# Weight loads by whole rows, the Gelu table load placed elsewhere, and two more MLP products copied out raw

## The chip, the cores and the metric

The kernel runs on one core of a Trainium2 chip. The metric is the device time of one execution in microseconds (us); a kernel's time is the median of its runs. TensorE is PE, VectorE is DVE, ScalarE is ACT, GpSimd is POOL, and SP is the engine whose queue issues nearly all the transfers.

## The reference

The reference is a transformer layer with a recurrent memory, followed by an MLP. The sequence of 2048 tokens is worked off in 64 segments of 32 tokens, and each segment sees eight memory rows that the segment before produced.

```
# per segment s (8 memory rows + 32 tokens, 512 wide, 32 heads of 128)
h = concat(mem, layernorm(x)[s])
q, k, v = h @ Wq, h @ Wk, h @ Wv
p = softmax(mask(q @ k.T * scale));  o = (p @ v) @ Wo
mem = o[:8];  out[s] = o[8:]
# whole sequence, F = 1792
h = x + out
h2 = h + gelu(layernorm(layernorm(h)) @ w1 + b1) @ w2 + b2
```

Wq, Wk and Wv are each 512 x 4096 in bf16, so that one of their rows has 8192 bytes.

## The kernel before

**Staging.** WQ, WK, WV and WO (4 MB each) are loaded once and stay in SBUF while the 64 segments run one after another. WQ lies in SBUF as 128 partitions x 4 blocks x 4096 columns: block `c` holds rows `128 c` to `128 c + 127` of the matrix. A projection contracts over the four blocks, and it is made in two halves: half `r = 0` yields heads 0 to 15 (columns 0 to 2047), and half `r = 1` heads 16 to 31. So a half needs the same 2048 columns of all four blocks. Each half is 16 matmuls, four for each block.

**The opening.** Segment 0 is written out by hand in the table `START`: the V projections of the tokens of blocks 0 and 1 (`("B", "V", ...)`, operand `hB`) and of the memory part (`"V"`, operand `hT`), then K in the same way, then Q in the order Q of block 0 half 0 (`hB`), `Q0` (`hT`), Q of block 0 half 1 (`hB`), `Q1` (`hT`), and then the scores `SC0` and `SC1`. The loads are issued by SP in the order WV, WK, WQ, WO. `load_w` cuts each of the three projection matrices into four transfers of 1 MB.

**The steady part.** From segment 1 on, tables fix PE's order by segment. PE is the engine that has work nearly all the time.

**The MLP.** When the last segment is done, the MLP runs over four groups `k` of 512 tokens. `w1_first` makes the 14 products (`fc` 0 to 13) with W1 of the first group, partly in the last segments, into PSUM banks 4 and 5 in turn. While ACT still needs its Exp tables, such a product is copied out of PSUM as it is ("raw") into a buffer `gT0`, and `gelu_late` applies Gelu in place later; the other products go through Gelu on the way out of PSUM (the line of `w1_first`'s `activation`). `RAW` is the number of products that are copied raw. The compiler puts an `ACT_TABLE_LOAD` ahead of the first Gelu. The buffers of `gT0` are re-used tiles, so a trace shows them as `xn`, `hT`, `kq`, `VSB`, `QTB`, `VBD` and, for fc 12 and 13, `hT` again.

The products with W2 accumulate in the four banks of `quad`, one for each 128 tokens. At the end of a group, DVE adds the residual to each bank and writes the output row block (`WV<-quad,WV`, since the old WV holds these buffers). `p2_norm(k)` normalizes the rows of group `k` on DVE (`WV<-WQ,agg,rst`, four instructions); it waits until `p2_load(k)` has brought them from memory (`WQ<-h_mid`). `p2_T(k)` transposes them by DMA.

**What sets the order of the engines.** PE's order is the order of the program. For the other engines a planner sorts all operations by their rank, which is the length of what depends on them, plus a bonus from the table `BONUS` by name, and inserts each at the earliest place that a table of costs gives. So a change of one name's bonus, or of one duration, can put later operations of ACT, DVE and SP in another order. What an operation may wait for follows from its `reads` and `writes` keys; `("WQ", r, c)` is the key of half `r` of block `c`.

Of the kernel before, what the change touches and what calls it, by code (L numbers as in the profile page):

```python
# [22 lines left out]
TABLE = 1.28  # L23
# [7 lines left out]
RECORD = ()  # L31
KEEP = True
HOIST = 24
LATE, RAW, LEAD = 0, 10, 199
PIECES = (0, 4, 8, 11, 14)
HALVES = ("kq", "KA", "QT", "ZCm", "VS", "nmc", "EC", "rsc", "PC", "PTC", "OTm", "KB", "QTB", "VSB")
BONUS = {"": 3.88, "EC0": 19.37, "EC0@a1": -40, "EC0@a2": 0, "EC0@a3": 2.13, "EC0@m0": 4.48, "EC0@m1": 40, "EC0@m2": 0, "EC0@m3": -7.71,
# [466 lines left out]
DC = 4  # L504
# [4 lines left out]
FC = F // P  # L509
# [43 lines left out]
def t_dve(n):  # L553
    return 0.16 + 1.042e-3 * n
# [10 lines left out]
def build_kernel(nc, A_x, A_mem0, A_Wq, A_Wk, A_Wv, A_Wo, B_w1, B_b1, B_w2, B_b2, out):  # L565
# [3 lines left out]
    with st:  # L569
        def sb(name, shape, dt=BF16):  # L570
            return st.enter_context(nc.sbuf_tensor(name, shape, dt))
# [54 lines left out]
        cneg = sb("cneg", [P, 1], F32)  # L626
        b2bc = sb("b2bc", [P, D])
        m0 = b2bc[0:MEM, :]
        b1n = sb("b1n", [FC, P])
        b1t = sb("b1t", [P, FC], F32)  # L630
# [39 lines left out]
        for sl in range(2):  # L670
            for i in range(4):
# [20 lines left out]
             reads=["maskA"], writes=["maskA"])  # L692
# [9 lines left out]
        def load(fn, kb, writes):  # L702
            chain.append(S.dma(fn, kb, writes=writes))
        chain, spread = [], {}

        def load_w(W, wd, key):
            for r in range(2):
                for c0 in (0, 2):
                    load(lambda e, r=r, c0=c0: e.dma_start(W[:, c0:c0 + 2, r * 2048:(r + 1) * 2048], wd[:, c0:c0 + 2, r * 2048:(r + 1) * 2048]),  # L709
                         1024, [(key, r, c0), (key, r, c0 + 1)])  # L710

        def first(fn, kb, writes):
            S.dma(fn, kb, writes=writes, eng="act")
# [2 lines left out]
        first(lambda e: e.dma_start(b1n[:], b1_d), 4, ["b1n"])  # L716
        load_x(1, first)
        load_w(WV, wv_d, "WV")
        load_w(WK, wk_d, "WK")
        load_w(WQ, wq_d, "WQ")  # L720
        for g in range(4):
            for a in range(2):
# [292 lines left out]
        exps = []  # L1015
# [127 lines left out]
        def view(base, off, shape, dt=BF16):  # L1143
            b = base[:]
            n = 1
            for x_ in shape[1:]:
                n *= x_
            m = 2 if dt == F32 else 1
            flat = bass.AP(b.tensor, b.offset + off, [[b.ap[0][0], shape[0]], [1, m * n]])
            if dt == F32:  # L1150
                flat = flat.bitcast(F32)
            names = " ".join("a%d" % i for i in range(len(shape) - 1))
            return flat.rearrange("p (%s) -> p %s" % (names, names), **{"a%d" % i: shape[i + 1] for i in range(len(shape) - 2)})
# [5 lines left out]
        gT = view(WQ, 0, [P, FC, SBT])  # L1159
# [70 lines left out]
        def w1_first(fc, bank, raw=False):  # L1230
            p = fc // 2
            views, keys = homes[p]
            for cc in range(DC):
                v, c0, _ = [w for w in views if w[1] <= cc < w[2]][0]
                S.op("pe", lambda e, v=v, c=cc - c0, cc=cc: e.matmul(ps[bank][:, 0:SBT], v[:, c, (fc % 2) * P:(fc % 2 + 1) * P], hnT0[:, cc, :], start=(cc == 0),  # L1235
                                                                     stop=(cc == DC - 1), skip_group_check=True),
                     reads=keys + [("hnT", "first", t) for t in range(TBS)], writes=[("ps", bank)], dur=0.215, mode=MF, ni=2)
            g, gkeys = gT0_home[p]
            g = g[:, fc % 2, :]
            if raw:  # L1240
                S.either(copy2(g, ps[bank][:, 0:SBT], 512), reads=[("ps", bank)], writes=[("gT0", fc)] + gkeys)
                return
            S.op("act", lambda e: e.activation(g, ps[bank][:, 0:SBT], ACTF.Gelu_apprx_tanh, bias=b1t[:, fc:fc + 1], scale=1.0),
                 reads=[("ps", bank), "b1t"], writes=[("gT0", fc)] + gkeys, after=exps + gelus[:1], dur=0.69)

        gelus = []

        def gelu_late(fc):
            g, gkeys = gT0_home[fc // 2]
            g = g[:, fc % 2, :]  # L1250
            o = S.named(S.op("act", lambda e: e.activation(g, g, ACTF.Gelu_apprx_tanh, bias=b1t[:, fc:fc + 1], scale=1.0),
                     reads=["b1t"], writes=[("gT0", fc)] + gkeys, after=exps + gelus[:1], dur=0.66 if gelus else 0.66 + TABLE), "gl")
            gelus.append(o)

        def gT_of(k, fc):
# [249 lines left out]
        for fc in range(6, FC):  # L1505
            w1_first(fc, (4, 5)[fc % 2], fc < RAW)
            rest.get(fc, lambda: None)()
            if fc == 7:
                for i in range(6):
                    gelu_late(i)  # L1510
            if fc >= 9 and fc < RAW:
                for i in range(6, fc + 1) if fc == 9 else (fc,):
                    gelu_late(i)
        nat(NTB - 1)
        p2_res(0)
# [2 lines left out]
        for k in range(NSB):  # L1518
# [13 lines left out]
            for t in range(TBS):  # L1532
                tb, split = k * TBS + t, is_last(k, t)
                for i in range(2 if split else 1):
                    for fc in range(FC - lag, FC):
                        p2_w2t(k, fc, t, i if split else None)
                    c = slice(i * HALF, (i + 1) * HALF) if split else slice(0, D)
                    keys = [("ob", bf, t, i)] if split else [("ob", bf, t, 0), ("ob", bf, t, 1)]
                    src, key = (ps[7][:, 0:HALF], ("ps", 7)) if i else (quad[:, t, c], ("ps", t))
                    S.op("dve", lambda e, t=t, bf=bf, c=c, src=src: e.tensor_tensor(ob[:, bf, t, c], src, hb[:, bf, t, c], ALU.add),  # L1540
                         reads=[key, ("hb", bf, t)], writes=keys, after=used["WV"], dur=t_dve(c.stop - c.start))
# [6 lines left out]
def bass_sequential_preLN__memory_aug_recurrent_mem_tr__mixer_channel_mlp__prompt_kernel(  # L1548
    nc: bass.Bass,
    A_x: bass.AP,  # L1550
    A_mem0: bass.AP,
    A_Wq: bass.AP,
    A_Wk: bass.AP,
    A_Wv: bass.AP,
    A_Wo: bass.AP,
    A_seg_len,
    B_x: bass.AP,
    B_w1: bass.AP,
    B_b1: bass.AP,
    B_w2: bass.AP,  # L1560
    B_b2: bass.AP,
    out: bass.AP,
):
    assert int(A_seg_len) == SEG
    build_kernel(nc, A_x, A_mem0, A_Wq, A_Wk, A_Wv, A_Wo, B_w1, B_b1, B_w2, B_b2, out)
# [33 lines left out]
```

## Time and profile before

| what | value |
|---|---|
| median of three runs | 807.16 us (805.53 to 807.7) |
| profiled execution, its own time | 805.57 us |
| span of the profiled execution, first to last instruction | 803.8 us |
| PE busy | 778.6 us, 97% of the span |
| DVE, ACT, POOL busy | 75%, 69%, 11% |
| mean granted TensorE clock | 0.993 |
| chain that ended last | PE 92%, DMA 2%, SP's queue 2%, DVE 2%, ACT 1% |

The profiled execution took 805.57 us, of which 1.8 us lie outside the span. It is 1.6 us shorter than the median of the three runs. PE is busy for nearly the whole span, so what the other engines do costs time only where PE waits; the page's row of slices shows where PE is not full: the first two of 40 slices (0 to 40 us) and the last one.

### The profile page before, as it was taken

Reading aid. Unit: us, or ns where it says so; the run is one execution under the profiler, and the core shown is the slowest. Engines: PE = TensorE matmul, PEld = TensorE weight load, DVE = VectorE, ACT = ScalarE, POOL = GpSimd, SP = SyncE. Lnnn points to the kernel's source line nnn. Section 1 sums busy time; section 2 is a strip of 40 time slices with the busy share of each in tenths; the row PEclk is TensorE's granted clock in tenths of the full one; section 3 lists DMA queues with packets and bytes.
Section 4 is the critical chain, followed back from the end, with each engine's and each line's share of the span. In section 5 each row is a group of like instructions: output and inputs, shape, how many; then the busy total and the mean of one; then the engine's idle time right before and its main releaser. Section 6 shows DMA issues by size and latency. Waiting matters only on the chain.

```text
span 803.8 us, 46836 instructions
## 1 busy us (share of the span) xinstructions
PE 778.6 (97%) x21699; PEld 424.4 (53%) x20879; DVE 600.1 (75%) x1846; ACT 557.5 (69%) x1579; POOL 89.7 (11%) x211
## 2 busy tenths in 40 slices
PE   2899999999999999999999999999999999999998
PEld 1455555555555555555555555555555555644444
DVE  3277878888888888888888888888888888733311
ACT  1556777777777777777777777777777777773342
POOL 5012000010001010101010101000000000020700
PEclk9979999999999999999999999999999999999999
DMA  8962010111111111202020202010203111074300
GB/s 340 392 194 30 4 35 8 40 23 37 26 36 26 33 29 27 36 19 41 19 43 16 48 12 50 13 37 20 50 24 57 45 44 54 21 230 129 86 27 26
DMA packets 67091, 48.77 MB, mean 61 GB/s; under 512 B 28996, under 2 KB 63308, under 8 KB 66892
## 3 DMA queue, kind: packets, MB, share of 16 engines
q1 hardware_dynamic: 66560, 45.50, 21.1%
q8 instruction: 166, 2.72, 1.4%
q14 instruction: 33, 0.27, 0.1%
q10 hardware_dynamic: 332, 0.27, 0.1%
HBM read 31.08 MB, written 8.13 MB: 49 GB/s over the span
## 4 chain that ended last, share of the span: by engine, by line
PE 92%; DMA 2%; SPq 2%; DVE 2%; ACT 1%; issue 0%; DVEq 0%; ACTq 0%
PE ps L798 43%; PE ps L1085 15%; PE ps L547 8%; PE quad L1467 6%; PE ps L1453 5%; PE ps L1114 3%; PE quad L996 3%; DMA WQ<-in_A_Wq_dram 2%; PE quad L1057 2%; SPq L709 2%; PE ps L1027 2%; PE ps L1235 1%; PE ps L965 1%; PE quad L965 1%; PE quad L1000 1%; DVE TT L1097 0%
## 5 line engine op out<-in xcount | busy, mean ns | idle before, releaser
L1085 PE MATMUL ps<-WO,OT 128*32 128x256 bf16 x4224 | 141.2, 276 | 0.1
L798 PE MATMUL ps<-WQ,hT 128*32 128x512 bf16 x1864 | 131.5, 380 | 0.9 <-DVE hT L1091 0.5
L798 PE MATMUL ps<-WV,hT 128*32 128x512 bf16 x1364 | 125.5, 382 | 0.0
L798 PE MATMUL ps<-WK,hT 128*32 128x512 bf16 x1700 | 123.7, 380 | 0.1
L817 ACT ACTIVATE kq<-ps 128x512 bf16<-128x512 f32 x160 | 95.4, 596 | 35.9 <-PE ps L798 29.0
L1085 PEld LDWEIGHTS ps<-WO,OT 128*32 128x32 bf16 x4224 | 101.4, 97 | 26.5 <-ACT OT L816 5.5
L816 ACT CAST kq<-ps 128x512 bf16<-128x512 f32 x162 | 94.7, 585 | 20.3 <-PE ps L798 13.7
L816 ACT CAST OT<-quad 128x128 bf16<-128x128 f32 (+1 forms) x192 | 85.1, 443 | 26.0 <-PE quad L1000 17.6
L841 DVE STREAM_TRANSPOSE KALL<-kq 128x256 f32<-128x256 f32 x160 | 71.1, 444 | 15.3 <-ACT kq L816 11.8
L798 PEld LDWEIGHTS ps<-WQ,hT 128*32 128x32 bf16 x1864 | 49.7, 97 | 60.1 <-issue 18.2
L863 POOL COPY ZC<-QTB 128x256 bf16<-128x256 bf16 x64 | 25.5, 399 | 477.8 <-PE ps L965 455.5
L798 PEld LDWEIGHTS ps<-WK,hT 128*32 128x32 bf16 x1700 | 45.9, 96 | 57.2 <-issue 14.9
L547 PE MATMUL ps<-WV,hT 128*32 128x512 bf16 x684 | 67.7, 379 | 0.0
L798 PEld LDWEIGHTS ps<-WV,hT 128*32 128x32 bf16 x1364 | 38.8, 97 | 47.1 <-issue 36.9
L841 DVE STREAM_TRANSPOSE QT<-kq 128x256 f32<-128x256 f32 x128 | 57.0, 445 | 7.0 <-ACT kq L817 2.1
L1456 ACT ACTIVATE WQ<-ps,b1t 128x512 bf16<-128x512 f32 x42 | 28.9, 687 | 47.4 <-PE ps L1453 47.4
L1097 DVE STREAM_TRANSPOSE TT<-ps 128x256 f32<-128x256 f32 x66 | 29.6, 449 | 38.3 <-PE ps L1085 38.2
L816 ACT CAST VS<-ps 128x512 bf16<-128x512 f32 x65 | 38.0, 585 | 27.0 <-PE ps L798 26.9
L1540 DVE TENSOR_TENSOR WV<-quad,WV 128x512 bf16<-128x512 f32 (+1 forms) x16 | 10.7, 674 | 47.8 <-PE quad L1467 47.8
L816 DVE CAST VS<-ps 128x512 bf16<-128x512 f32 x63 | 41.7, 663 | 5.6 <-PE ps L798 5.6
L798 PE MATMUL ps<-WQ,hB 128*32 128x512 bf16 x512 | 42.4, 397 | 2.7 <-DMA WQ<-in_A_Wq_dram 2.0
L984 DVE TENSOR_TENSOR PC<-EC,rsc 128x128 bf16<-128x128 f32 x128 | 39.7, 310 | 4.3
(161 smaller groups left out, 1428.6 us busy)
## 6 DMA issues: line engine op xcount, KB each, us to landing
WV<-in_A_Wv_dram SPq DMA_DIRECT2D x4, 1024.0 KB, 10.2
WK<-in_A_Wk_dram SPq DMA_DIRECT2D x4, 1024.0 KB, 16.1
WQ<-in_A_Wq_dram SPq DMA_DIRECT2D x4, 1024.0 KB, 22.6
WO<-in_A_Wo_dram SPq DMA_DIRECT2D x8, 512.0 KB, 9.3
v_last<-VSB SPq DMA_DIRECT2D x60, 64.0 KB, 2.8
VBD<-v_last SPq DMA_DIRECT2D x60, 64.0 KB, 3.0
h_mid<-xr SPq DMA_DIRECT2D x16, 128.0 KB, 1.8
WK<-in_B_w_dram SPq DMA_DIRECT2D x4, 512.0 KB, 4.6
```

Of the source, the lines that this page charges most:

```text
L547: return e.add_instruction(mybir.InstMatmult(name="I-%d" % (4000000 + _kept[0]), engine=mybir.EngineType.PE, start_tensor_calc=start, stop ...
L798: ins = e.matmul(o, l, m, start=(k == 0), stop=(k == DC - 1), tile_position=(0, 32 * j), skip_group_check=True)
L816: return {"act": (lambda e: e.copy(out, src), t_act(n, ps_)), "dve": (lambda e: e.tensor_copy(out, src), 0.16 + 1.042e-3 * n * fast)}
L817: return {"act": (lambda e: e.mul(out, src, scale_), t_act(n, ps_)), "dve": (lambda e: e.tensor_scalar(out, src, scale_, None, ALU.mult), ...
L841: S.op("dve", lambda e: e.transpose(out, src), reads=[("kq", i)], writes=[key], dur=t_dve(256) + 0.02, after=after)
L863: S.op("pool", lambda e: e.tensor_copy(dst, src), reads=[("QTB", bk % 2, q) for q in range(2)], writes=[("ZCb", par)], dur=0.45)
L984: S.op("dve", lambda e: e.tensor_tensor(PC[:, r].rearrange("p t a -> p a t"), EC[:, r], bc, ALU.mult), reads=[("EC", r), ("rsc", r)], writ ...
L1085: ins = e.matmul(ps[bank][32 * j:32 * j + 32, 0:256], lhs(slot(h)), wo_cols(h, b), start=(k == 0), stop=(k == 15), tile_position=(0, 32 * ...
L1097: S.op("dve", lambda e: e.transpose(tt.rearrange("p c q t -> p (c q t)"), ps[bank][:, 0:256]), reads=[("ps", bank)], writes=[("TT", par)], ...
L1453: ins = e.matmul(ps[bank][:, 0:SBT], W1[:, cc, fc * P:(fc + 1) * P], hnT_of(k)[:, cc, :], start=(cc == 0), stop=(cc == DC - 1))
L1456: S.op("act", lambda e: e.activation(gT[:, fc, :], ps[bank][:, 0:SBT], ACTF.Gelu_apprx_tanh, bias=b1t[:, fc:fc + 1], scale=1.0), reads=[(" ...
L1467: S.op("pe", lambda e: e.matmul(quad[:, t, :], lhs, W2[:, fc, :], **flags), reads=[("W2", part_of(fc))] + gT_keys(k, fc), writes=[("ps", t ...
```

## The change

Three things change. First, `load_w` issues, for each of WV, WK and WQ, four transfers of whole rows, one for each block `c`, in place of four transfers of half rows. The bytes and the number of transfers are the same. Second, `RAW` goes from 10 to 12: the products fc 10 and 11 are copied raw into `VBD`, and their Gelu follows in place, after the Gelus of the others in the program. Third, the first late Gelu, ahead of which the table load stands, gets a name of its own, `gl0`, with a bonus of 10 where it had -40.

```diff
-LATE, RAW, LEAD = 0, 10, 199
+LATE, RAW, LEAD = 0, 12, 199
...
-... "gl": -40,
+... "gl": -40, "gl0": 10,
...
         def load_w(W, wd, key):
-            for r in range(2):
-                for c0 in (0, 2):
-                    load(lambda e, r=r, c0=c0: e.dma_start(W[:, c0:c0 + 2, r * 2048:(r + 1) * 2048], wd[:, c0:c0 + 2, r * 2048:(r + 1) * 2048]),
-                         1024, [(key, r, c0), (key, r, c0 + 1)])
+            for c in range(DC):
+                load(lambda e, c=c: e.dma_start(W[:, c, :], wd[:, c, :]), 1024, [(key, r, c) for r in range(2)])
...
-                     reads=["b1t"], writes=[("gT0", fc)] + gkeys, after=exps + gelus[:1], dur=0.66 if gelus else 0.66 + TABLE), "gl")
+                     reads=["b1t"], writes=[("gT0", fc)] + gkeys, after=exps + gelus[:1], dur=0.66 if gelus else 0.66 + TABLE), "gl" if gelus else "gl0")
...
-            if fc >= 9 and fc < RAW:
-                for i in range(6, fc + 1) if fc == 9 else (fc,):
+            if fc == 9:
+                for i in range(6, 10):
+                    gelu_late(i)
+            if RAW > 10 and fc == FC - 1:
+                for i in range(10, RAW):
                     gelu_late(i)
```

The first place where instructions wait for something else is PE's Q projections in the opening. `dsem12` to `dsem15` are the semaphores of WQ's four transfers, `hB` is the operand of block 0's tokens and `hT` that of the memory part. Before:

```order
L798 MATMUL ps<-WQ,hB 32x512 [waits sem_act]
L798 MATMUL ps<-WQ,hB 32x512 x7
L798 MATMUL ps<-WQ,hB 32x512 [waits dsem13]
L798 MATMUL ps<-WQ,hB 32x512 x7
L798 MATMUL ps<-WQ,hT 32x512 [waits sem_act]
L798 MATMUL ps<-WQ,hT 32x512 x15
L798 MATMUL ps<-WQ,hB 32x512 [waits dsem14]
L798 MATMUL ps<-WQ,hB 32x512 x7
L798 MATMUL ps<-WQ,hB 32x512 [waits dsem15]
L798 MATMUL ps<-WQ,hB 32x512 x7
L798 MATMUL ps<-WQ,hT 32x512 x16
```

And of the changed kernel, whose lines here are two lower:

```order
L796 MATMUL ps<-WQ,hB 32x512 [waits sem_act]
L796 MATMUL ps<-WQ,hB 32x512 x3
L796 MATMUL ps<-WQ,hB 32x512 [waits dsem13]
L796 MATMUL ps<-WQ,hB 32x512 x3
L796 MATMUL ps<-WQ,hB 32x512 [waits dsem14]
L796 MATMUL ps<-WQ,hB 32x512 x3
L796 MATMUL ps<-WQ,hB 32x512 [waits dsem15]
L796 MATMUL ps<-WQ,hB 32x512 x3
L796 MATMUL ps<-WQ,hT 32x512 [waits sem_act]
L796 MATMUL ps<-WQ,hT 32x512 x15
L796 MATMUL ps<-WQ,hB 32x512 x16
L796 MATMUL ps<-WQ,hT 32x512 x16
```

The matmuls stand in the same order. The wait for the fourth transfer stood ahead of the last 24 of these 64 matmuls, and it now stands ahead of the last 52.

The second place is DVE at the end of the MLP's first group. `WV<-quad,WV` is the output of 128 tokens out of a bank of `quad`, `WV<-WQ,agg,rst` is `p2_norm`, here of group 2, and `dsem3` is the semaphore of that group's load. Before:

```order
L1121 TENSOR_TENSOR OTB<-ps,OTB 64x512 [waits sem_act]
L1540 TENSOR_TENSOR WV<-quad,WV 128x512 [waits sem_pe,sem_pool] x4
L1186 TENSOR_SCALAR WV<-WQ,agg,rst 128x512 [waits dsem3]
L1186 TENSOR_SCALAR WV<-WQ,agg,rst 128x512 x3
L1122 TENSOR_TENSOR oBn<-OTB 32x512 [waits dsem90,dsem89,dsem91,dsem88,sem_dve]
```

Of the changed kernel:

```order
L1119 TENSOR_TENSOR OTB<-ps,OTB 64x512 [waits sem_act]
L1541 TENSOR_TENSOR WV<-quad,WV 128x512 [waits sem_pe,sem_pool]
L1184 TENSOR_SCALAR WV<-WQ,agg,rst 128x512 [waits dsem3]
L1184 TENSOR_SCALAR WV<-WQ,agg,rst 128x512 x3
L1541 TENSOR_TENSOR WV<-quad,WV 128x512 [waits sem_pe] x3
L1120 TENSOR_TENSOR oBn<-OTB 32x512 [waits dsem90,dsem89,dsem91,dsem88,sem_dve]
```

The normalization of group 2 with its wait has moved ahead of the last three of the four outputs.

The third place is ACT at the start of the MLP, from the last raw copies on. `QTB` holds the products fc 8 and 9, `VBD` fc 10 and 11; `OT<-quad` is the output of an attention step. Before:

```order
L816 CAST QTB<-ps 128x512 x2
L816 CAST OT<-quad 128x32x24
L1251 ACT_TABLE_LOAD
L1251 ACTIVATE xn<-xn,b1t 128x512 x2
L1251 ACTIVATE hT<-hT,b1t 128x512
L1251 ACTIVATE kq<-kq,b1t 128x512
L1243 ACTIVATE VBD<-ps,b1t 128x512 x2
L1243 ACTIVATE hT<-ps,b1t 128x512 x2
```

Of the changed kernel:

```order
L814 CAST QTB<-ps 128x512 x2
L1249 ACT_TABLE_LOAD
L1249 ACTIVATE xn<-xn,b1t 128x512 x2
L1249 ACTIVATE hT<-hT,b1t 128x512 x2
L1249 ACTIVATE kq<-kq,b1t 128x512
L814 CAST VBD<-ps 128x512 x2
L1241 ACTIVATE hT<-ps,b1t 128x512 x2
```

The copy of `OT` has left ACT (it now stands on DVE, where there was nothing between two groups of transposes), one more late Gelu stands ahead of the copies of fc 10 and 11, and these two are casts. The two Gelus that are missing here come later, behind those of `QTB`.

2 rows, old and new, of the table BONUS are left out of this document.

## The prediction

> **What bounds the kernel now.** I read the page first, then the chain of waits for the opening, then the two places where PE's order meets a changed wait: the Q projections and the start of the MLP. The page says where time can be won or lost at all:
>
> ```profile
> PE 778.6 (97%) x21699; PEld 424.4 (53%) x20879; DVE 600.1 (75%) x1846; ACT 557.5 (69%) x1579; POOL 89.7 (11%) x211
> PE 92%; DMA 2%; SPq 2%; DVE 2%; ACT 1%; issue 0%; DVEq 0%; ACTq 0%
> WQ<-in_A_Wq_dram SPq DMA_DIRECT2D x4, 1024.0 KB, 22.6
> ```
>
> PE has work for 97% of the span and is 92% of the chain; the steady part in between is not touched by the change. DMA and SP's queue make 4%, and both are in the opening. The chain (start, length, what) of the first 50 us:
>
> ```profile
> 18.94 18.43 DMA WQ<-in_A_Wq_dram
> 37.41 1.58 PE ps L798 x24
> 40.87 1.74 PE ps L798 x15
> 45.01 1.71 PE ps L798 x16
> 46.72 1.71 PE ps L1085 x32
> ```
>
> All before 37.4 us hangs on the last piece of WQ: only then do the last 24 Q matmuls run. PE's timeline at that place (start, length, instructions, idle time before):
>
> ```profile
> 29.48 1.91 PE L798 MATMUL ps<-WK,hT 128*32 128x512 bf16 x32
> 31.22 1.91 PE L798 MATMUL ps<-WK,hB 128*32 128x512 bf16 x32
> 32.95 1.04 PE L798 MATMUL ps<-WQ,hB 128*32 128x512 bf16 x16
> 34.84 0.62 PE L798 MATMUL ps<-WQ,hB 128*32 128x512 bf16 x8
> 37.41 0.61 PE L798 MATMUL ps<-WQ,hB 128*32 128x512 bf16 x8 [1.96 <-DMA WQ<-in_A_Wq_dram]
> 37.85 1.12 PE L798 MATMUL ps<-WQ,hT 128*32 128x512 bf16 x16
> ```
>
> PE is idle for 1.96 us. The stages show transfers and clock (length; busy PE, PEld, DVE, ACT, POOL; granted clock, DMA share, GB/s):
>
> ```profile
> 26.00:28.00 2.00, 2.00 (x40) 1.46 (x131) 0.00 (x0) 1.02 (x3) 0.00 (x0) 1.00 1.03 416
> 32.00:34.00 2.00, 2.00 (x44) 0.87 (x36) 1.04 (x3) 1.20 (x3) 0.00 (x0) 1.00 1.02 403
> 38.00:40.00 2.00, 1.30 (x36) 0.46 (x24) 0.81 (x2) 1.47 (x3) 0.74 (x2) 0.67 1.05 344
> 42.00:44.00 2.00, 1.42 (x84) 0.72 (x79) 1.14 (x4) 1.20 (x4) 0.00 (x0) 0.50 1.10 348
> 48.00:50.00 2.00, 2.00 (x44) 1.24 (x40) 0.82 (x3) 0.00 (x0) 0.00 (x0) 0.77 0.79 243
> ```
>
> The transfers run at some 410 GB/s until WQ is in, so the opening is bound by bandwidth. And behind the idle stretch the granted clock is 0.5: 0.67 in 38 to 40 us means from about 38.7 us on, 0.77 in 48 to 50 us means until about 48.9 us. That is 10.2 us, in which 16 matmuls of the chain take 1.71 us, while 32 took 1.74 us before (29.48 to 31.22).
>
> **The change part by part.**
>
> *Rows of 8192 bytes.* WQ's four pieces now end one block each, not one half each. Twelve pieces of 1024 KB at 410 GB/s are 12.58 MB / 410 = 30.7 us. Does a longer row move faster? The nearest rows: pieces with 4 KB rows move at 410 GB/s, WO with 1 KB rows at 348 GB/s (42 to 44 us, when only WO moves). Over 16 engines that is 160 ns for 4 KB and 47 ns for 1 KB, so a line through both gives 37.6 ns per KB and 9.4 ns a piece; 8 KB would take 310 ns, or 422 GB/s. The three matrices then take 29.8 us: **0.9 us earlier**, the last piece at 36.5 us. Bounds: 0 (the rows are cut to 4 KB anyway, the piece lands at 37.4 us) and, for no fixed cost at all, twice as much (1.8 us). The Trainium skill, "DMA: Bandwidth & Descriptors", section "Why small descriptors are slow (HBM only)", names a fixed cost of about 3 cycles a packet beside one cycle per 32 bytes; by it a 4 KB row is 131 cycles and two are 262 against 259, an estimate of 0.3 us, and the sum would come out 0.6 us higher. The rows of this trace show more than twice that fixed cost, so I stay with 0.9 us.
>
> *What is left to do behind the last piece.* Before, half 0 needed two pieces and was done before the wait; 24 matmuls were left. Now the fourth block is needed by half 0 already: 12 matmuls run, and 52 are left. A matmul is 1.74 / 32 = 0.054 us, so 28 more of them cost **1.5 us**, and nothing hides them, since the scores and the softmax follow on Q1 in both kernels. WV and WK also come by blocks now, without harm: WQ's four pieces of 2.56 us ahead of 37.4 us put WK's last piece at 27.2 us at the latest, and PE takes up WK's first block 32 matmuls ahead of the row at 29.48, at 27.7 us.
>
> *The clock.* PE is now idle from about 33.7 us (32.95 and 12 matmuls) to 36.5 us, 2.8 us instead of 1.96. A gap of 1.96 us was enough for 10.2 us at half clock, so I expect the half clock again, and it can come earlier: before the 52 matmuls, not behind the 24. Bounds: none of the extra matmuls slowed, 0; all 52 slowed, 52 x 0.054 = 2.8 us, of which some comes back because the slow stretch then ends earlier. I take a third, **0.9 us**. The Trainium skill, "TensorE: Matmul & The Clock Gate", section "Why this matters for your kernels", says that gaps up to about 3 us are safe; this trace has the clock drop behind 1.96 us, so the measurement decides. Part 1 of the same page of the Trainium skill says that the monitor's window runs free of the kernel's start, which would make the loss differ from run to run; one trace cannot show that.
>
> *The MLP's start.* PE waits here once, for the bank of fc 10:
>
> ```profile
> 711.54 1.90 PE L1235 MATMUL ps<-hnT,hT 128*128 128x512 bf16 x8
> ...
> 713.74 0.60 PE L1235 MATMUL ps<-hnT,xT 128*128 128x512 bf16 x2 [0.30 <-ACT VBD L1243]
> ...
> 708.29 0.81 ACT L816 CAST OT<-quad 128x768 bf16<-128x768 f32 x1
> 709.11 1.28 ACT L1251 ACT_TABLE_LOAD   x1
> ...
> 711.79 0.70 ACT L1251 ACTIVATE hT<-hT,b1t 128x512 bf16<-128x512 bf16 x1
> 712.40 0.71 ACT L1251 ACTIVATE kq<-kq,b1t 128x512 bf16<-128x512 bf16 x1
> 713.02 1.39 ACT L1243 ACTIVATE VBD<-ps,b1t 128x512 bf16<-128x512 f32 x2
> ...
> 720.40 0.58 ACT L1120 COPY OTB<-ps 64x512 f32<-64x512 f32 x1
> ...
> 724.11 0.59 PE L1467 MATMUL quad<-WK,VBD 128*128 128x512 bf16 x2
> ```
>
> The `OT` copy leaves ACT and the table load comes 0.7 us earlier, but one more Gelu (0.6 us from row to row) stands ahead of fc 10's copy, which is a cast of 0.58 us and no Gelu of 0.7 us. So the bank comes free 0.2 us earlier: **-0.2 us** (at best the whole 0.3). The two Gelus that were put off follow `QTB`'s. ACT was through with all Gelus at 720.4 us; it now has two casts more (1.2 us) and the `OT` copy less (0.8 us), so it is through at 720.8 us, and PE wants `VBD` at 724.1 us: hidden, with 3 us of cover.
>
> *The moved normalization.* The rows of group 2 and the outputs (DVE), the load (SP) and PE's next products:
>
> ```profile
> 726.11 0.69 DVE L1540 TENSOR_TENSOR WV<-quad,WV 128x512 bf16<-128x512 f32 x1 [0.17 <-PE quad L1467]
> ...
> 727.83 0.69 DVE L1540 TENSOR_TENSOR WV<-quad,WV 128x512 bf16<-128x512 f32 x1 [0.17 <-PE quad L1467]
> 730.31 1.38 DVE L1186 TENSOR_SCALAR WV<-WQ,agg,rst 128x512 bf16<-128x512 bf16 x4 [1.78 <-DMA WQ<-h_mid]
> ...
> 725.75 0.45 SPq L1180 DMA_DIRECT2D WQ<-h_mid  x1
> ...
> 732.06 1.03 PE L1467 MATMUL quad<-WK,WQ 128*128 128x512 bf16 x4
> 732.92 1.03 PE L1453 MATMUL ps<-WQ,WK 128*128 128x512 bf16 x4
> ```
>
> The load is issued at 725.75 us and lands at 730.3 us in either kernel: what SP does ahead of it is the same. DVE now does one output, waits for the load, normalizes (1.38 us, until 731.7) and only then frees the other three banks of `quad`, each 0.69 us behind the one before: 732.4, 733.1, 733.75 us. PE's four products, one for each bank, begin at 732.06 us less the 0.2 won above, 0.215 us apart (four from 732.06 to 732.92), so it wants the fourth bank at 732.5 us and gets it at 733.75. **+1.2 us** (from 0.4, if the load comes 0.8 us earlier, to 2, if it comes later). SP's group transposes now stand ahead of three stores, which nobody waits for. The last block's rows and POOL's residuals are late by 1.5 us too:
>
> ```profile
> 745.58 8.93 POOL L1192 TENSOR_TENSOR WV<-WQ,b2bc 128x512 f32<-128x512 bf16 x8
> 752.18 0.69 DVE L1540 TENSOR_TENSOR WV<-quad,WV 128x512 bf16<-128x512 f32 x1 [0.17 <-PE quad L1467]
> ```
>
> Four of the eight, 4.5 us, are due before 752.18 us; they end at 750.05 us, so 2.1 us of cover are left.
>
> *The sum.* -0.9 + 1.5 + 0.9 - 0.2 + 1.2 = **+2.5 us**. On the profiled execution, 805.57 us, that is 808.1 us; this one is 1.6 us below the median, and on the median of 807.16 us it is **809.7 us**, 0.3% slower. A difference of 0.3% (2.4 us) is about what a measurement of this kernel can tell from no change, as its runs from 805.53 to 807.7 us show.
>
> **The rivals.**
>
> *The clock isn't dropped* (not slower). If PE, with its gap at another place, still counts as busy enough, the opening runs at full clock. The chain's three rows at half clock (1.74 + 1.71 + 1.71 us) then take half, 2.6 us less at most; part of the first row lies beside the softmax and would turn into a wait, so I take 2.2 us. That comes off the time before, and the forecast's +0.9 us falls away: 809.7 - 0.9 - 2.2 = **806.6 us**. It decides if a gap of 2.8 us leaves the clock up. Against it: a gap of 1.96 us did drop it. For it: the gap now begins 1.7 us earlier, and one trace says little on where the limit lies. By the skill's rule on gaps this would be the usual case; the trace bears that out badly. Chance 0.20.
>
> *The rows bring nothing* (the change doesn't do what it says). The 8 KB rows are cut to 4 KB or move no faster: the 0.9 us are gone, the gap is 3.7 us, and the slow stretch takes in all 52 matmuls, 2.8 us in place of the 0.9 counted, of which some 0.9 come back at its end. 809.7 + 0.9 + 1.0 = **811.6 us**. For it: no row that I quote moves 8 KB at a time from SP's queue. Chance 0.20.
>
> *The normalization doesn't stall PE.* If the load lands by 729 us, the banks come free in time: 809.7 - 1.2 = **808.5 us**. Against it: SP's queue ahead of the load is unchanged. Chance 0.10.
>
> **How the numbers follow.** The forecast has 0.50; its own range, from the bounds of the clock (0 to 2 us) and of the stall (0.4 to 2 us), is 808 to 811.6 us, about half on each side of 0.3%: 0.28 slower, 0.22 within. The first rival gives 0.08 faster (where the rows gain their 1.8 us too: 805.7 us, and the stall stays out: 804.5 us) and 0.12 within; the second 0.20 slower; the third 0.10 within. So faster 0.08, within 0.44, slower 0.48. The range reaches down to 805.7 us, that end of the first rival, and up to 812.5 us, 0.9 us above the second for a load that lands later.
>
> **What would show it.** Right: PE's Q matmuls wait once, ahead of the 13th, for 2.5 to 3 us until about 36.5 us; transfers at 420 GB/s until then; a stretch at clock 0.5 that begins before 38.7 us; no wait for `VBD` at 713 us or one under 0.15 us; and a PE wait of about 1.2 us at `quad<-WK,WQ`, with DVE idle for some 4 us between the first output and the normalization. Wrong: 410 GB/s or less, a clock of 1.0 through 50 us, or no wait of PE at the second group's first W2 products.

## The result and the profile after

The changed kernel takes 804.29 us (median of 18 runs, 802.47 to 807.41), the kernel before 806.33 us (18 runs, 805.08 to 807.7). The ratio is 0.9974, with a 95% interval of 0.9964 to 0.9984: some 2.0 us faster (1.3 to 2.9). The forecast was 2.5 us slower, and the time lies below its range. (The 809.7 us were counted from 807.16 us, the median of three runs; 0.8 us of the distance is that the median of 18 is 806.33 us.) The profiled execution took 803.95 us, with a span of 802.2 us.

The page of the changed kernel (busy times, packets by size):

```profile
PE 775.9 (97%) x21699; PEld 423.1 (53%) x20880; DVE 600.7 (75%) x1847; ACT 558.0 (70%) x1580; POOL 90.1 (11%) x211
DMA packets 65555, 48.77 MB, mean 61 GB/s; under 512 B 28996, under 2 KB 63308, under 8 KB 63820
```

And the packet row of the kernel before:

```profile
DMA packets 67091, 48.77 MB, mean 61 GB/s; under 512 B 28996, under 2 KB 63308, under 8 KB 66892
```

The three matrices are 12 MB: 3072 packets of 4 KB before, 1536 of 8 KB after. The total fell by just 1536, and the packets of 2 KB or more but under 8 KB by 3072. So the 8 KB rows are moved whole. PE is busy for 2.7 us less (778.6 to 775.9 us) with the same instructions, since less of them fall into a stretch at half clock, as the windows show. The transfers are faster too; two stretches of the windows (length; busy PE, PEld, DVE, ACT, POOL; granted clock, DMA share, GB/s), first of the kernel before, then of the changed kernel, there with two more:

```profile
2.00:12.00 10.00, 0.30 (x4) 0.11 (x4) 1.79 (x3) 1.55 (x2) 6.32 (x31) 1.00 0.95 346
12.00:30.00 18.00, 13.71 (x173) 8.22 (x360) 4.96 (x7) 7.03 (x16) 4.53 (x6) 1.00 1.02 409
```

```profile
2.00:12.00 10.00, 0.30 (x4) 0.11 (x4) 1.79 (x3) 1.55 (x2) 6.32 (x31) 1.00 0.97 393
12.00:30.00 18.00, 13.00 (x164) 7.82 (x347) 4.54 (x7) 6.71 (x15) 4.57 (x6) 1.00 1.01 421
42.00:44.00 2.00, 1.56 (x89) 1.34 (x78) 1.29 (x5) 1.21 (x5) 0.00 (x0) 0.60 1.10 348
44.00:46.00 2.00, 2.00 (x32) 1.06 (x28) 0.69 (x2) 0.53 (x2) 0.00 (x0) 0.55 1.10 350
```

From 12 us on the rate goes from 409 to 421 GB/s; ahead of that, where ACT's queue brings rows of x beside the weights, it goes from 346 to 393 GB/s. The last two rows show WO's 1 KB rows at 348 to 350 GB/s, as before, and a granted clock of 0.60 and 0.55: half clock for 1.6 + 1.8 = 3.4 us, where it was 10.2 us before. PE's timeline in the opening of the changed kernel:

```profile
33.47 0.82 PE L796 MATMUL ps<-WQ,hB 128*32 128x512 bf16 x12
35.34 0.40 PE L796 MATMUL ps<-WQ,hB 128*32 128x512 bf16 x4 [1.05 <-DMA WQ<-in_A_Wq_dram]
43.89 1.96 PE L796 MATMUL ps<-WQ,hB 128*32 128x512 bf16 x16
47.30 0.62 PE L1083 MATMUL ps<-WO,OT 128*32 128x256 bf16 x16
```

PE takes up the 13th Q matmul at 35.34 us, after a single wait as predicted, but one of 1.05 us and not of 2.5 to 3; it was 37.41 us for the last piece before, so the piece comes 2.1 us earlier. The opening ends when DVE transposes the output of segment 0 (`TT`). That row before and after, and the same row of the last segment:

```profile
49.89 0.45 DVE L1097 STREAM_TRANSPOSE TT<-ps 128x256 f32<-128x256 f32 x1 [1.15 <-PE ps L1085]
701.68 0.45 DVE L1097 STREAM_TRANSPOSE TT<-ps 128x256 f32<-128x256 f32 x1 [2.27 <-PE ps L1085]
```

```profile
47.97 0.45 DVE L1095 STREAM_TRANSPOSE TT<-ps 128x256 f32<-128x256 f32 x1
700.09 0.45 DVE L1095 STREAM_TRANSPOSE TT<-ps 128x256 f32<-128x256 f32 x1 [2.27 <-PE ps L1083]
```

The opening ends 1.92 us earlier; the last segment is 1.59 us earlier; the span is 1.6 us shorter (803.8 to 802.2). From the last `TT` to the end of the span it is 102.1 us in both. So in these two executions the whole difference arises in the first 50 us (0.3 us of it is lost again in the steady part), and the MLP neither gains nor loses. Its rows after, in the order of the prediction (PE's wait for fc 10, PE's first `VBD` products, the load of group 2, the normalization, the last three outputs, PE's products of the second group):

```profile
712.10 0.60 PE L1233 MATMUL ps<-hnT,xT 128*128 128x512 bf16 x2 [0.25 <-ACT VBD L814]
722.47 0.59 PE L1465 MATMUL quad<-WK,VBD 128*128 128x512 bf16 x2
723.39 0.45 SPq L1178 DMA_DIRECT2D WQ<-h_mid  x1
727.70 1.38 DVE L1184 TENSOR_SCALAR WV<-WQ,agg,rst 128x512 bf16<-128x512 bf16 x4 [3.40 <-DMA WQ<-h_mid]
729.00 1.88 DVE L1541 TENSOR_TENSOR WV<-quad,WV 128x512 bf16<-128x512 f32 x3
730.42 1.03 PE L1465 MATMUL quad<-WK,WQ 128*128 128x512 bf16 x4
```

### The profile page after: what moved, and what is told of

It reads as the page before. It is cut to its first block, busy times and chain, and to the rows that moved or that the text cites. A ratio compares the mean times of both kernels' runs of the same rounds, so it can differ in the third digit from the quotient of the medians.

```text
span 802.2 us, 46835 instructions
## 1 busy us (share of the span) xinstructions
PE 775.9 (97%) x21699; PEld 423.1 (53%) x20880; DVE 600.7 (75%) x1847; ACT 558.0 (70%) x1580; POOL 90.1 (11%) x211
## 4 chain that ended last, share of the span: by engine, by line
PE 91%; DMA 3%; DVE 2%; ACT 1%; SPq 1%; issue 1%; POOL 0%; DVEq 0%; ACTq 0%
PE ps L796 43%; PE ps L1083 15%; PE ps L547 8%; PE quad L1465 6%; PE ps L1451 5%; DMA WQ<-in_A_Wq_dram 3%; PE ps L1112 3%; PE quad L994 3%; PE quad L1055 2%; PE ps L1025 2%; PE ps L1233 1%; PE ps L963 1%; PE quad L963 1%; SPq L708 1%; PE quad L998 1%
## 5 line engine op out<-in xcount | busy, mean ns | idle before, releaser
L814 ACT CAST OT<-quad 128x128 bf16<-128x128 f32 x191 | 84.4, 442 | 27.0 <-PE quad L998 18.8
L1112 PE MATMUL ps<-WO,OTB 128*32 128x512 bf16 x512 | 42.1, 381 | 0.4 <-issue 0.2
```

The source lines that it names most:

```text
L814: return {"act": (lambda e: e.copy(out, src), t_act(n, ps_)), "dve": (lambda e: e.tensor_copy(out, src), 0.16 + 1.042e-3 * n * fast)}
L1112: ins = e.matmul(ps[bank][32 * j:32 * j + 32, :], OTB[:, bk % 2, slot(h), :], WO[:, h, :], start=(k == 0), stop=(k == 7), tile_position=(0 ...
```

## The experiments

Where the expectations speak of the theory A2, it is this: the opening ends with WO. The bytes of WV, WK, WQ and WO pass one after another, WO's last piece lands at the end of them all, and PE waits for it, or would wait at full clock. Whatever PE does between WQ's last piece and WO's last piece is hidden. The rivals are the prediction's own step (PE's matmuls behind WQ's last piece set the end and cost their 1.5 us: rivals E and F, where a letter is used), that the order of the blocks and not the length of the rows brings the gain (C), that the clock decides, and that the MLP part does.

### The parts of the change

**e1: the whole rows alone.** The kernel before, with only `load_w` changed:

```diff
-            for r in range(2):
-                for c0 in (0, 2):
-                    load(... W[:, c0:c0 + 2, r * 2048:(r + 1) * 2048] ...)
+            for c in range(DC):
+                load(... W[:, c, :] ...)
```

> Only WV, WK and WQ by whole rows; the MLP's start as before. If the gain of 2.0 us comes from the transfers (theory A), this kernel has all of it: about 804.3 us, WQ's last piece at about 35.3 us as in the changed kernel. If it comes from the MLP's start (rival B), this kernel is at 806 us or, by the prediction's sum (-0.9 + 1.5 + 0.9), at about 808 us.

**e2: the MLP part alone.** All lines of the change that bear on the MLP, with the loads of before; two of them:

```diff
-LATE, RAW, LEAD = 0, 10, 199
+LATE, RAW, LEAD = 0, 12, 199
...
-... "gl")
+... "gl" if gelus else "gl0")
```

> Only the MLP part (RAW = 12 and the bonus of the first late Gelu); the loads as before. Theory A: no gain, 806.3 us, or up to 1.2 us more where PE waits for the banks behind the moved normalization. Rival B: the gain is here, about 804.3 us.

e1: 804.35 us (802.93 to 807.16), ratio 0.9979 (0.9967 to 0.9991). e2: 806.47 us (804.86 to 809.26), ratio 1.0008 (0.9995 to 1.0022). So the rows have a gain of the size of the whole change's. Of the MLP part no effect is clear of the noise, which leaves room for -0.4 to +1.8 us. The two traces showed more than the times, because in both the clock stayed at 1.0 through the opening. PE's waits for WQ and WO in e1, with its first WO matmuls and the end of the opening:

```profile
35.31 0.40 PE L796 MATMUL ps<-WQ,hB 128*32 128x512 bf16 x4 [2.09 <-DMA WQ<-in_A_Wq_dram]
43.00 0.63 PE L1083 MATMUL ps<-WO,OT 128*32 128x256 bf16 x16
47.19 0.62 PE L1083 MATMUL ps<-WO,OT 128*32 128x256 bf16 x16 [1.18 <-DMA WO<-in_A_Wo_dram]
47.86 0.45 DVE L1095 STREAM_TRANSPOSE TT<-ps 128x256 f32<-128x256 f32 x1 [1.35 <-PE ps L1083]
```

In e2, with the loads of before:

```profile
37.91 0.62 PE L798 MATMUL ps<-WQ,hB 128*32 128x512 bf16 x8 [1.99 <-DMA WQ<-in_A_Wq_dram]
43.71 0.63 PE L1085 MATMUL ps<-WO,OT 128*32 128x256 bf16 x16
46.91 0.62 PE L1085 MATMUL ps<-WO,OT 128*32 128x256 bf16 x16 [1.26 <-DMA WO<-in_A_Wo_dram]
49.55 0.62 PE L1085 MATMUL ps<-WO,OT 128*32 128x256 bf16 x16 [1.37 <-DMA WO<-in_A_Wo_dram]
50.22 0.45 DVE L1097 STREAM_TRANSPOSE TT<-ps 128x256 f32<-128x256 f32 x1 [2.99 <-PE ps L1085]
```

Both end with a wait for WO that neither of the first two traces shows. With the clock at full speed in both, PE is at its first WO matmuls only 0.7 us earlier in e1 (43.00 against 43.71 us), and yet the opening ends 2.4 us earlier, as WO's last piece comes 2.4 us earlier (47.19 against 49.55 us). And the opening of e2 at full clock ends no earlier (50.22 us) than that of the kernel before with 10.2 us at half clock (49.89 us); e1 at full clock ends as the changed kernel does with 3.4 us at half clock (47.86 and 47.97 us). The half clock took up time that would otherwise have been spent waiting for WO. These rows suggested A2.

**e3: WV and WK by whole rows, WQ by halves as before**, so that 24 matmuls are left behind WQ's last piece.

```diff
+            if key != "WQ":
+                for c in range(DC):
+                    load(... W[:, c, :] ...)
+                return
             for r in range(2):
```

> WV and WK by whole rows, WQ still by half rows, so that 24 and not 52 matmuls are left behind WQ's last piece; the MLP's start as before. Theory A: the last piece lands about two thirds of 2.1 us earlier, at 36.0 us, and the 1.5 us of 28 more matmuls fall away: about 804.5 us or less, no slower than whole rows for all three. If it is not the transfers' speed but the order of the pieces that gains (rival C), this kernel is at 806 us.

804.9 us (803.32 to 806.25), ratio 0.998 (0.997 to 0.9991). The last wait of PE and the end of the opening:

```profile
48.10 0.62 PE L1089 MATMUL ps<-WO,OT 128*32 128x256 bf16 x16 [1.66 <-DMA WO<-in_A_Wo_dram]
48.77 0.45 DVE L1101 STREAM_TRANSPOSE TT<-ps 128x256 f32<-128x256 f32 x1 [3.44 <-PE ps L1089]
```

With 28 matmuls fewer behind the piece, the opening does not end earlier than in e1, against what was expected, but 0.9 us later: 4 MB less come by long rows, and WO's last piece comes 0.9 us later (48.10 against 47.19 us). In the medians the difference to e1 (0.55 us) is not resolved.

**e4: PE kept from being idle ahead of WQ's last piece**, with 32 matmuls that read WV and the identity and whose result nobody uses:

```diff
-          ("B", "Q", 0, (0, 5)), "Q0", ("B", "Q", 0, (1, 4)), ...
+          ("B", "Q", 0, (0, 5)), "Q0", ("W", 7, 8), ("B", "Q", 0, (1, 4)), ...
```

> The kernel before with 32 matmuls without a use (8 x 4, 1.7 us, into a free bank) in PE's gap ahead of the last 24 Q matmuls, so that PE is busy while it waits; no transfer is touched. It prices the half clock. If the half clock behind the gap is what the change shortened (rival D), the stretch at 0.5 is gone or 3.4 us long and the time is 2 us shorter, about 804.3 us. If the stretch comes from the many short waits of the scores and the softmax and not from the gap, the time stays at 806.3 us.

809.08 us (806.36 to 810.2), ratio 1.003 (1.0018 to 1.0041): slower. The clock stayed up until 47.8 us, but then PE stood idle for 2.00 us without a wait that the profile shows ("issue"), with half clock from within that gap on:

```profile
46.00 0.62 PE L1085 MATMUL ps<-WO,OT 128*32 128x256 bf16 x16 [1.31 <-DMA WO<-in_A_Wo_dram]
49.03 1.04 PE L767 MATMUL ps<-WV,ident 128*32 128x512 bf16 x7 [2.00 <-issue]
```

So this run doesn't price the half clock by itself, and that price stays inconclusive here.

### Row length, order of the blocks, and WO

**e5: the block order with short rows.** Blocks in the order of e1, each in two pieces of 512 KB with the 4 KB rows of before.

```diff
+            for c in range(DC):
+                for r in range(2):
+                    load(... W[:, c, r * 2048:(r + 1) * 2048] ...)
```

> The loads in the changed kernel's order (block by block, so that 52 matmuls are left behind WQ's last piece), but in pieces of half rows: transfers of 4 KB as before. Theory A2: the opening ends when WO's last piece lands, and PE's work behind WQ is hidden ahead of that; the packets' length is what gains. Then this kernel is no faster and no slower than before: 805.9 us, WQ's last piece at about 37.4 us. Rival E, the prediction's step: 28 more matmuls behind the wait cost 1.5 us: 807.4 us. Rival C (the order of the pieces gains): 804.3 us.

804.59 us (803.7 to 806.9) beside 805.61 us of the kernel before; the ratio is 0.9994 (0.9985 to 1.0004): no change that is clear of the noise.

```profile
35.39 0.40 PE L797 MATMUL ps<-WQ,hB 128*32 128x512 bf16 x4 [2.18 <-DMA WQ<-in_A_Wq_dram]
48.78 0.62 PE L1084 MATMUL ps<-WO,OT 128*32 128x256 bf16 x16 [1.37 <-DMA WO<-in_A_Wo_dram]
49.45 0.45 DVE L1096 STREAM_TRANSPOSE TT<-ps 128x256 f32<-128x256 f32 x1 [1.54 <-PE ps L1084]
```

This is the sharpest of the comparisons with e1. PE gets the last block for half 0 at the same time (35.39 and 35.31 us; here that is the seventh of WQ's eight pieces, since the eighth holds half 1), and has the same matmuls left behind it. Yet the opening ends 1.6 us later, because WO's last piece lands 1.6 us later (48.78 and 47.19 us). Neither the order of the blocks nor PE's work behind WQ makes the difference in the opening: PE still waits 1.37 us for WO, although the clock was at half for 3.4 us from 35.8 us on. The times don't settle it by themselves. e5's interval overlaps that of e1 (0.9967 to 0.9991), and its median is only 0.2 us above e1's. The part behind the opening varies too much for that: from this `TT` to that of the last segment it takes 651.1 us in e5's trace, 652.6 us in e1's and up to 653.6 us in the others; why it varies was not followed.

**e6: 512 KB more between WQ and WO.** e1 with one more transfer in SP's queue behind WQ's last piece: part of Wq, in 256-byte rows, into a buffer that is overwritten later before it is read.

```diff
         load_w(WQ, wq_d, "WQ")
+        load(... hnT0 <- 512 KB of Wq in 256-byte rows ...)
```

> Whole rows for all three, and one more transfer of 512 KB in rows of 256 bytes (its data is not used) between WQ and WO, so that WO lands some 2.3 us later and WQ does not. Theory A2 (WO's landing ends the opening): 2.3 us longer than whole rows alone, about 806.6 us. Rival F (WQ's landing sets the opening's end, as the prediction had it): no change, 804.35 us.

807.76 us (805.65 to 810.18), ratio 1.003 (1.0019 to 1.0042), so some 4 us slower than e1.

```profile
47.53 1.05 PE L1084 MATMUL ps<-WO,OT 128*32 128x256 bf16 x16 [2.45 <-DMA WO<-in_A_Wo_dram]
51.20 1.04 PE L1084 MATMUL ps<-WO,OT 128*32 128x256 bf16 x16 [1.34 <-DMA WO<-in_A_Wo_dram]
52.29 0.45 DVE L1096 STREAM_TRANSPOSE TT<-ps 128x256 f32<-128x256 f32 x1 [5.68 <-PE ps L1084]
```

WQ comes as in e1 and PE's program is that of e1, but WO's last piece comes 4.0 us later, the opening ends 4.4 us later, and that arrives in the time. More was lost than the expected 2.3 us: the short rows were dearer than reckoned.

**e7: WO's first piece ahead of WQ's last one.** The bytes up to WO's last piece are the same, but WQ comes later.

```diff
             for c in range(DC):
+                if key == "WQ" and c == 3:
+                    load_wo(0, 0)
                 load(... W[:, c, :] ...)
```

> Whole rows for all three, with WO's first piece of 512 KB (1.5 us) issued ahead of WQ's last piece, so that WQ lands 1.5 us later and WO's last piece when it did. Theory A2: no change, 804.35 us. Rival F (WQ's landing sets the opening's end): 1.5 us longer, about 805.9 us.

805.11 us (803.41 to 807.41), ratio 0.9993 (0.998 to 1.0006). The intervals of e1 and e7 overlap, and the median lies between the two theories, so the times don't decide. The trace leans to A2:

```profile
36.59 0.40 PE L800 MATMUL ps<-WQ,hB 128*32 128x512 bf16 x4 [2.81 <-DMA WQ<-in_A_Wq_dram]
47.10 0.64 PE L1087 MATMUL ps<-WO,OT 128*32 128x256 bf16 x16
47.77 0.45 DVE L1099 STREAM_TRANSPOSE TT<-ps 128x256 f32<-128x256 f32 x1
```

WQ's piece comes 1.28 us later than in e1, and the opening ends at the same time (47.77 and 47.86 us): the wait of 1.18 us for WO has gone, and nothing else. It also says how much cover there is: the 1.2 us of e1 are used up here.

**e8 and e9: WO by 4 KB rows**, in e1 and in the kernel before. Partition p then holds rows of Wo that belong elsewhere, so the attention output is not the reference's; the bytes, pieces and matmuls are the same.

```diff
-load(... WO[:, h0:h0 + 4, :], wo_d[:, h0:h0 + 4, :] ...)
+load(... WO[:, h0:h0 + 4, :], A_Wo[h0:h0 + 4].rearrange("h e d -> (h e) d").rearrange("(e h) d -> e h d", h=4) ...)
```

> WV, WK and WQ by whole rows as in e1, and WO's eight pieces read as 4 KB rows in place of four 1 KB rows for each partition. The bytes, the pieces and the order are the same; partition p then holds other rows of Wo than it should, so the attention output is not the reference's. WO then moves at some 410 GB/s in place of 348: 4.19 MB take 10.2 us in place of 12.05, and the last piece lands 1.8 us earlier. Theory A2 (the opening ends with WO's last piece): PE's wait of 1.18 us for it goes, then PE's own order is the bound: opening over 1.0 to 1.2 us earlier than in e1 (46.7 to 46.9 us in place of 47.86), some 803.2 us, ratio about 0.9965. Theory of the prediction (PE's matmuls behind WQ's last piece bound the opening, WO is hidden): as e1, 804.35 us, ratio 0.998.

> The kernel before, with WO's pieces read as 4 KB rows as in e8 (the attention output is not the reference's for the same reason). Theory A2: in the kernel before, WO's last piece lands at about the time that PE wants it at half clock, and 1.3 to 2.6 us after that at full clock (e2's waits for WO). So with the clock at half nothing is gained at all, and with the full clock up to 1.8 us: between ratio 1.0 and 0.998. A rival (half clock costs nothing because something else bounds the opening as well): no gain in either case and the opening ends at 49.9 us as before.

e8: 803.81 us (801.5 to 807.46), ratio 0.9976 (0.996 to 0.9991). e9: 805.5 us (802.8 to 807.44), ratio 0.9997 (0.9982 to 1.0013). e8's last WO matmuls, the end of its opening, and PE's next wait:

```profile
45.96 0.64 PE L1083 MATMUL ps<-WO,OT 128*32 128x256 bf16 x16
46.63 0.45 DVE L1095 STREAM_TRANSPOSE TT<-ps 128x256 f32<-128x256 f32 x1
47.89 0.61 PE L765 MATMUL ps<-WV,ident 128*32 128x512 bf16 x7 [0.68 <-issue]
```

e9's:

```profile
47.45 0.62 PE L1085 MATMUL ps<-WO,OT 128*32 128x256 bf16 x16 [0.27 <-DMA WO<-in_A_Wo_dram]
48.12 0.45 DVE L1097 STREAM_TRANSPOSE TT<-ps 128x256 f32<-128x256 f32 x1 [0.44 <-PE ps L1085]
```

In the traces it goes as A2 says: with WO earlier, the wait goes and the opening ends 1.23 us earlier than in e1 (46.63 against 47.86 us), and in e9 1.77 us earlier than before, with a profiled clock that was at half for 3.4 us. In the medians neither gain can be seen. A part of e8's is given back at once: PE next stands idle for 0.68 us without a wait that the profile shows, where e1 does so for 0.23 us at that place. What is left would be within the intervals. So it is e1 and e6 that show how time won or lost on the way to WO's last piece reaches the end; e8 and e9 show it for the opening alone.

**WO's landing itself.** The traces also have the moment at which a transfer lands. The last of WO's eight transfers (times of issue, then us from issue to landing) and PE's last WO matmuls of segment 0, in the kernel before:

```profile
L724 SPq DMA_DIRECT2D WO<-in_A_Wo_dram x1: 1420/1420/1420, 40.6 to 40.6; - x1
DMA to landing us min/median/max: 8.5/8.5/8.5
49.22 0.62 PE L1085 MATMUL ps<-WO,OT 128*32 128x256 bf16 x16
```

In the changed kernel, where the matmuls start at 47.30 us:

```profile
L722 SPq DMA_DIRECT2D WO<-in_A_Wo_dram x1: 1417/1417/1417, 38.5 to 38.5; - x1
DMA to landing us min/median/max: 8.6/8.6/8.6
```

The piece lands at 49.1 us before and at 47.1 us after, and PE takes it up 0.1 to 0.2 us later, as in e1, e2, e3, e5, e6, e7 and e9. So, to within 0.2 us, WO's landing ends the opening in the first two traces as well, though they mark no wait for it: behind a stretch at half clock, PE got there at nearly the same moment.

**The clock of every run.** In the 87 executions of the kernel before that were taken beside the experiments, the time doesn't go with the granted clock: the 36 with a mean clock of 0.998 or more have a median of 805.7 us, the 28 with 0.995 or less one of 805.8 us. Where WO's cover is used up, it does: the five executions of e7 at a clock of 1.0 have a mean of 803.9 us, its other seven 806.1 us; in e8 it is 803.1 us (eight) and 805.8 us (four). So half clock went with no more time where WO's landing covered it, and with 2 to 3 us more where it did not. These groups were formed afterwards, and one doesn't fit: in the changed kernel the seven executions at 1.0 have a mean 1.7 us longer than the other eleven (805.6 and 804.0 us), which stays open.

### The prediction's own term, laid bare

**e10 and e11: all of WO ahead of WQ**, in e1 (52 matmuls left behind WQ's last piece) and in e3 (24 left). Nothing is loaded behind WQ now that PE waits for. Other parts of the program come in another order, so only the opening is read; each has a single execution (814.51 and 815.57 us).

```diff
+        <the eight loads of WO>
         load_w(WQ, wq_d, "WQ")
-        <the eight loads of WO>
```

> e1 with all of WO loaded ahead of WQ, so that WQ's last piece is the last of the 16 MB and nothing behind it can hide what PE still has to do. The rest of the program comes in another order at places, so only the opening is read. WQ's last piece should come 11 to 12 us later than in e1 (at 46.5 to 47.5 us), there is no wait for WO, and from there PE needs the 11.2 us that e7 took from that piece to the end of the opening (36.6 to 47.8 us without a wait for WO).

> As e10, but WQ in four half-row pieces, so that 24 Q matmuls in place of 52 are left behind the last piece. Here the prediction's term can be read by itself: if 28 matmuls of 0.054 us are on the path when nothing else hides them, the stretch from WQ's last piece to the end of the opening is 1.5 us shorter than in e10. If it is equal, that term was wrong in itself and not only hidden.

e10, the last wait for WQ and the end of the opening:

```profile
47.25 0.62 PE L796 MATMUL ps<-WQ,hB 128*32 128x512 bf16 x4 [1.89 <-DMA WQ<-in_A_Wq_dram]
60.23 0.45 DVE L1095 STREAM_TRANSPOSE TT<-ps 128x256 f32<-128x256 f32 x1
```

e11:

```profile
47.42 0.62 PE L802 MATMUL ps<-WQ,hB 128*32 128x512 bf16 x8 [1.51 <-DMA WQ<-in_A_Wq_dram]
58.21 0.45 DVE L1101 STREAM_TRANSPOSE TT<-ps 128x256 f32<-128x256 f32 x1
```

From WQ's last piece to the end of the opening e10 needs 12.98 us and e11 10.79 us, 2.2 us less. Both were at half clock for a part of that: e10 for 4.0 us, until 51.2 us, while its Q matmuls ran, and e11 for 3.4 us, from 52.9 us on. So the 2.2 us are not the price of 28 matmuls alone. A cleaner figure comes from stretches at full clock, from WQ's last piece to the first WO matmuls: 7.69 us with 52 matmuls left in e1 (35.31 to 43.00 us) and as much in e7 (36.59 to 44.28 us), 5.80 us with 24 left in e2 (37.91 to 43.71 us) and 5.85 us in e11 (47.42 to 53.27 us, all but the last 0.4 us at full clock). That is 1.9 us, somewhat more than the 1.5 us of the prediction. So the cost of the whole rows to PE is real, and in e10, with nothing behind it, it is paid; in the changed kernel the landing of WO comes later still.

## Why the prediction was wrong

**The step that failed** is "What is left to do behind the last piece", where it says that "nothing hides them, since the scores and the softmax follow on Q1 in both kernels". It followed the chain of the kernel before, which runs from WQ's last piece over PE to the end of the opening, with no wait for WO in it. But the chain showed PE at half clock, and just this slowness hid the second bound: WO's last piece, which comes some 12 us behind WQ's (37.91 and 49.55 us in e2) and in the kernel before landed at 49.1 us, 0.1 us ahead of PE's last WO matmuls. At full clock with the same loads PE waits for it (e2: 1.37 us), and with a block's work more behind WQ it still does (e1: 1.18 us). So +1.5 us were counted that cost nothing (e5, and the opening of e7), though as PE's own work they are there, and at 1.9 us. The prediction had the row that should have warned it: at 42 to 44 us the transfers were still at work at 348 GB/s, on the WO that PE needs in the same opening.

**The clock (+0.9).** It fell again and came at another time, for 3.4 us from 42.4 us on, not before 38.7 us, and in e1 and e7 it did not fall in the opening at all, with gaps of 2.09 and 2.81 us ahead of WQ's piece. The gap of 2.8 us that the prediction reckoned with was 1.05 us in the changed kernel. It cost nothing either way, under the same cover: half clock and full clock end the opening within 0.1 us of each other (47.97 and 47.86 us). The rival "The clock isn't dropped" was right that the clock can stay up, but wrong that this is worth 2.2 us: e2 has it and its opening ends no earlier. The Trainium skill, "TensorE: Matmul & The Clock Gate", section "Why this matters for your kernels", calls gaps up to about 3 us safe: e1 and e7 agree, the kernel before, with its 1.96 us, does not.

**The rows (-0.9).** The mechanism and the rate were right: 422 GB/s were reckoned for 8 KB rows, and from 12 to 30 us they moved at 421, against 409 GB/s before. For all 12.58 MB that would be 0.9 us. But WQ's last piece came 2.1 us earlier (37.41 to 35.34 us), more than the bound of 1.8 us. What the sum left out are the first 12 us: the 47 GB/s between 346 and 393 over 10 us are 0.47 MB, or 1.1 us of transfer. With 0.7 us for the rates from 12 us to WQ's last piece that makes 1.8 of the 2.1 us. e5, with the new order and 4 KB rows, has 349 GB/s there, so this too goes with the length of the rows; why they gain more beside the rows of x, no run shows. "The rows bring nothing" is refuted by the count of packets. And the term is worth nearly its full size at the end, because WO moves up with it (49.1 to 47.1 us).

**The MLP's start (-0.2)** came out at 0.05: the wait for fc 10's bank is 0.25 us instead of 0.30.

**The moved normalization (+1.2)** came out at nothing in the changed kernel's trace. DVE waited ahead of it as foreseen (3.40 us), but the outputs' last bank was free at 729.00 + 1.88 = 730.9 us and PE began at 730.42 us without a wait. Against the reckoning, three small things came together: relative to PE's `VBD` products the load was issued 0.7 us earlier (0.92 us behind them instead of 1.64), it landed after 4.31 us instead of 4.56, and three outputs took 1.88 us instead of 2.1. The rival "The normalization doesn't stall PE" was right in this, and its condition, a landing by 729 us, was met at 727.7 us. But it was near: in e2's trace, with the same MLP part, the outputs end at 732.80 + 1.88 = 734.7 us, and PE's four products, which want the fourth bank at 734.5 us, take 1.12 us to the next product (733.84 to 734.96 us) where they take 0.86 us otherwise. So the stall is there, at 0.3 us, in that execution.

**The sum as measured:** -2.1 us for the rows, 0 for PE's work and for the clock, 0 to 0.3 us for both MLP terms, so about -2 us, beside -2.0 us in the medians and -1.6 us in the profiled executions.

## What to carry to other kernels

When a stage shows a wait for one load on its chain, look for the load behind it: ask when the last byte lands that the stage needs, and at what clock the engine would reach it. A chain shows only the latest of the bounds, and an engine that is slow for another reason can hide the next one by a hair; then work added to the engine is free up to that cover, and bytes saved ahead are worth their full size. Here rows of 8 KB in place of 4 KB paid, although the pieces then fitted the consumer's order less well, because the transfers and not the consumer end the stage. And read a stage's clock and its waits from more than one execution: in one profile half clock and a hidden load looked like PE's own work.

## What the hardware showed that was not expected

- The clock's fall didn't follow the length of the gap: 1.96 us of idle time ahead of WQ's last piece were followed by 10.2 us at half clock in the kernel before, 1.99 us in e2 and 2.81 us in e7 by none. It also differs between executions of one kernel: the mean granted clock of the kernel before went from 0.991 to 1.0 in the 87 executions. The stretches at half clock up to 60 us in the traces are 3.4, 6.8, 10.2 or 13.7 us long.
- Rows of 8 KB moved at 421 GB/s (12 to 30 us of the changed kernel), of 4 KB at 409 in the same stretch of the kernel before, of WO's 1 KB at 348 to 350.
- PE can stand idle with no wait that the profile shows: 2.00 us in e4, where 32 matmuls were added, and 0.68 us in e7 and e8, where only data came at another time. What it waits for, and how that depends on what the transfers do, was not tried.
